# Attention and bilinear FFN on one core: Strassen for part of the first batch element, wider weight combinations, and probability sums made by accumulating transfers

## The chip, the cores and the metric

The kernel runs on one core of a Trainium2 chip. The metric is the time of one execution on the device, in microseconds, as the median of several runs. The profile is of one execution; its span is a little shorter than the time, since it begins with the first instruction that it shows.

In what follows PE is TensorE, DVE is VectorE, ACT is ScalarE, POOL is GpSimd and SP is the engine that issues most transfers. SBUF is the core's working memory, PSUM the memory into which PE writes.

## The reference

Four batch elements, eight heads, 768 positions, head size 64. Queries and keys are each put into one of 16 clusters by their largest cosine with the head's centroids, and a query attends only to keys of its own cluster. The result, 3072 rows of 512, goes through a bilinear feed-forward layer (FFN).

```python
q_assign = argmax(q_n @ c_n.T); k_assign = argmax(k_n @ c_n.T)
scores = where(q_assign == k_assign, q @ k.T / 8, -1e9)
x = softmax(scores) @ v              # (4, 8, 768, 64) -> (3072, 512)
out = (x @ w_a) * (x @ w_b) @ w_out  # 512 -> 1536 -> 512
```

The three FFN weights come as 64-bit floats and are turned into 32-bit ones on the core.

## The kernel before

**Attention.** Heads are worked on in pairs, 16 pairs in all, four per batch element (HP = 4). A pair has two halves of 384 queries (hf), and each half six units, one for each block of 128 keys (j = 0 to 5). A group, counted by g, is two units. For each group `score` makes both units' scores in PSUM (L554) and ACT takes the exponential into a tile pt (L563; four pt buffers, so a unit's exp overwrites the pt of four units earlier). In the next group `add_up` sums the probabilities of the half into a tile acc (L585), and `weigh` multiplies pt by v (L596). One or two groups after a half is complete, `denominators` sums acc over its partitions by a matmul with ones (L619), and `normalize` takes the reciprocal and multiplies it onto xT, the transposed attention output of the batch element (L653). In the first four pairs DVE makes all sums of `add_up` but the last block's, which PE takes in; in the other twelve POOL makes those of one head and the later ones of the other.

**FFN.** Once a batch element's xT is complete, `ffn_ready` puts its FFN, cut into pieces, into the queue `ffn`. The main loop over groups takes as many pieces per group as a credit of PE columns allows (PER_GROUP), and whatever is left runs after the last group. A piece's matmuls go through `in_halves` (L679), which makes two matmuls of 64 columns each. The up-projections of the last three batch elements use Strassen's scheme in Winograd's form (`ffn_ups`): seven products in place of eight for each pair of f-tiles (128 columns of w_a or w_b), from combinations of x (T1 to T4, `combine_x`) and of the weights (S1 to S4, L783, made by DVE one chunk of 128 at a time). ACT copies a product out of PSUM (L815), DVE adds further ones (L818), POOL multiplies the a and b sides (L824). The first batch element's up-projections are plain (`ffn_block`): each f-tile and half of the positions takes four chunks of 128 of the inner dimension. The down-projections use Strassen for all four.

**Weights.** 36 parts of 128x512 are loaded as 64-bit raw tiles (two buffers) and rounded by `round_w`: four DVE passes (L280 to L290) build a leading part and a rest, POOL adds them (L295), ACT takes the absolute value of the upper word (L294), and `flush_w` sets very small weights to zero on DVE (L302). `due` gives the group in which each part is rounded: eight in groups 1 to 22, the others from group 23.

**Order.** The order of instructions on each engine is the order in which the program is written; nothing is rescheduled. Small steps of `normalize` and of the next pair's preparation wait in the queue `todo` and are taken one after each FFN piece. A flag computed at the end decides whether a slow path (`long_path`) does everything again; with these inputs it doesn't run.

Of the kernel before, what the change touches and what calls it, by code (L numbers as in the profile page):

```python
# [28 lines left out]
SMALLEST = 1.125 * 2.0 ** -15  # L29

# [5 lines left out]
def kernel(  # L36
# [97 lines left out]
    with tc.If(redo > 0):  # L134
        with ExitStack() as slow:
            long_path(nc, tc, slow, c, q, k, v, out)


def short_path(nc, tc, ctx, c, cn, centroids_in, casts, n_far, q, k, v,
# [32 lines left out]
    sizep = pool("sizep", 2)  # L172
# [96 lines left out]
    flush = []  # L269

    def round_w(i):
        flush_w()
# [18 lines left out]
                                       in1=rest, op0=ALU.mult, op1=ALU.mult)  # L291

        size = sizep.tile([P, WN], FP32, name="size")
        nc.scalar.activation(out=size, in_=halves(FP32)[:, :, 1], func=AF.Abs)  # L294
        nc.gpsimd.tensor_tensor(out=w, in0=w, in1=rest, op=ALU.add)  # L295
        flush.append((w, size))

    def flush_w():

        while flush:  # L300
            w, size = flush.pop(0)
            nc.vector.scalar_tensor_tensor(out=w, in0=size, scalar=SMALLEST,  # L302
                                           in1=w, op0=ALU.is_ge, op1=ALU.mult)

    stat = zero.tile([P, 4 * NPAIR], FP32, name="stat")
# [151 lines left out]
    def prep_by_blocks(p):  # L457
# [47 lines left out]
        if p == HP:  # L505
            return [[lambda: across(0), lambda: across(1)], [sims_across],
                    assign[:2], assign[2:], [one_hot, one_hot_across], []]
# [3 lines left out]
    def prep_steps(p):  # L511
# [6 lines left out]
        if by_blocks(p):  # L518
            steps = prep_by_blocks(p)
            ready = [lambda s=s: todo.extend(s) for s in steps]  # L520
            ready[1] = both(lambda: prep_sim(p), lambda: load_v(p), steps[1][0],
                            lambda: todo.extend(steps[1][1:]))
            return ready
# [50 lines left out]
    def add_up(u):  # L574
        p, hf, j = where(u)
        if j == 0 or j == NJ - 1 and p < HP:
            return
        if j == 1:
            accs[p, hf] = accp.tile([P, 2, HB], FP32, name="acc")
        acc = accs[p, hf]  # L580
        for a in range(2):

            many = p >= HP and (a == 1 or j > 3)
            eng = nc.gpsimd if many else nc.vector
            eng.tensor_tensor(  # L585
                out=acc[:, a, :],
                in0=probs[u - 1][:, a, :] if j == 1 else acc[:, a, :],
                in1=probs[u][:, a, :], op=ALU.add)
# [39 lines left out]
    def normalize(p, hf):  # L628
# [21 lines left out]
        def apply():  # L650

            eng = nc.vector if (p, hf) == (HP - 1, 0) else nc.gpsimd
            eng.tensor_tensor(out=x, in0=x, in1=den, op=ALU.mult)  # L653
            unchecked.append((4 * p + 2 * hf + 1, inv))

        return [across, invert, back, apply]

    def check_inverses():
        while unchecked:
            n, inv = unchecked.pop()  # L660
            nc.scalar.activation(out=inv, in_=inv, func=AF.Copy,
                                 accum_out=stat[:, n:n + 1])

# [24 lines left out]
    def ffn_block(b, blk):  # L688

        box = {}  # L690
        t0 = blk * HB

        def up(w_sb, f):
            ps = in_turn()
            for ch in range(NCH):
                in_halves(ps[:, 0:HB], w_sb[:, ch, f * P:(f + 1) * P],
                          xTs[b][:, ch, t0:t0 + HB],
# [3 lines left out]
        def piece_a(f):  # L701
            if f == 0:
                box["h"] = hp_.tile([P, NF, HB], FP32, name="h")
            ps = up(wa_sb, f)
            box["a"] = hap.tile([P, HB], FP32, name="ha")
            nc.scalar.copy(out=box["a"], in_=ps[:, 0:HB])

        def piece_b(f):
            ps = up(wb_sb, f)
            nc.vector.tensor_tensor(out=box["h"][:, f, :], in0=box["a"],  # L710
                                    in1=ps[:, 0:HB], op=ALU.mult)

        ups = [(NCH * HB, lambda f=f, piece=piece: piece(f))
               for f in range(NF) for piece in (piece_a, piece_b)]
        return ups, box
# [11 lines left out]
    def room():  # L727
        if not W:
            W["raw"] = [rawp.tile([P, 2 * WN], FP32, name="raw") for _ in range(2)]
            W["size"] = [sizep.tile([P, WN], FP32, name="size") for _ in range(2)]  # L730
            W["comb"] = combp.tile([P, 2 * P], FP32, name="comb")
        return W["raw"], W["size"], W["comb"]
# [4 lines left out]
    def up_room():  # L737
        raw, size, comb = room()
        quarter = lambda t: t[:, 0:2 * HB].rearrange("p (c t) -> p c t", c=2)
        beside = lambda t: t[:, 2 * HB:].rearrange("p (c f) -> p c f", c=2)  # L740
        chunks = lambda t: [t[:, c, :] for c in range(2)]
        W["T3"], W["T2"] = chunks(quarter(raw[0])), chunks(quarter(raw[1]))
        W["T4"] = [t[:, 0:HB] for t in size]
        W["slots"] = [chunks(beside(raw[0])), chunks(beside(raw[1])),
                      chunks(comb.rearrange("p (c f) -> p c f", c=2)),
                      [t[:, HB:] for t in size]]

    def combine_x(b, c):
        if c == 0:
            up_room()  # L750
        x = xTs[b]
        x11, x12 = x[:, c, 0:HB], x[:, c, HB:S]
        x22 = x[:, c + 2, HB:S]
        t2, t3 = W["T2"][c], W["T3"][c]
        for out, l, r in ((t3, x22, x12), (x12, x12, x11), (t2, x22, x12)):
            nc.vector.tensor_tensor(out=out, in0=l, in1=r, op=ALU.subtract)

    def ffn_ups(b, h):

        x = xTs[b]  # L760
        X = {"11": [x[:, c, 0:HB] for c in (0, 1)],
             "T1": [x[:, c, HB:S] for c in (0, 1)],
             "21": [x[:, c, 0:HB] for c in (2, 3)],
             "22": [x[:, c, HB:S] for c in (2, 3)]}

        def combine_t4():
            for c in range(2):
                nc.vector.tensor_tensor(out=W["T4"][c], in0=X["21"][c],
                                        in1=W["T2"][c], op=ALU.subtract)

        def products(w_sb, i, is_a):
            N2 = NF // 2
            A = {m + n: [w_sb[:, c, f * P:(f + 1) * P] for c in cs]
                 for m, f in (("1", i), ("2", i + N2))
                 for n, cs in (("1", (0, 1)), ("2", (2, 3)))}
            box = {}

            def combine(name, l, r, op):
# [3 lines left out]
                for c in range(2):  # L782
                    nc.vector.tensor_tensor(out=dst[c], in0=l[c], in1=r[c], op=op)  # L783
# [16 lines left out]
            def product(name, l, r, start=True):  # L800
                ps = box[name]
                rhs = X[r] if r in X else W[r]
                for c in range(2):
                    in_halves(ps[:, 0:HB], A[l][c], rhs[c],
# [8 lines left out]
            def take(name, k, f):  # L813
                box[name] = place(k, f)
                nc.scalar.copy(out=box[name], in_=box["X"][:, 0:HB])  # L815

# [55 lines left out]
        parts = [products(w_sb, i, w_sb is wa_sb) for i in range(NF // 2)  # L872
                 for w_sb in (wa_sb, wb_sb)]
        pieces = []
        for n, (combinations, ps) in enumerate(parts):
            if n == 0:
                ps[0] = both(*combinations, ps[0])
                ps[2] = both(combine_t4, ps[2])
# [4 lines left out]
        return pieces  # L883
# [9 lines left out]
    def ffn_downs(b, h):  # L893
# [97 lines left out]
        def before():  # L991
            down_room()
# [19 lines left out]
    blocks = {}  # L1012

    def ffn_ready(p, hf):

        b, hp = divmod(p, HP)
        if hp < HP - 1:
            return
        if b > 0:
            if hf == 0:  # L1020
                return
            h = []
            for c in range(2):
                ffn.insert(len(ffn) - FREE_ROOM + c, (0, lambda c=c: combine_x(b, c)))
            ffn.extend(ffn_ups(b, h) + ffn_downs(b, lambda: h))
        elif hf == 0:
            blocks[0] = ffn_block(0, 0)
            ffn.extend(blocks[0][0][0:8])
        else:
            ups0, box0 = blocks[0]  # L1030
            ups, box = ffn_block(0, 1)
            for n in range(3):
# [370 lines left out]
```

## Time and profile before

| | |
|---|---|
| time, median of 3 | 1044.93 us (1044.05 to 1045.06) |
| span of the profile | 1042.1 us |
| PE busy | 1030.8 us |
| DVE busy | 658.7 us |
| ACT busy | 302.8 us |
| POOL busy | 334.1 us |
| transfers | 46.49 MB, 18.7% of the 16 DMA engines' span on the main queue |

Busy times of different engines overlap. A group row of the profile gives line, engine, operation, output and inputs, shapes and count, then the busy time of the whole group, the mean of one in ns, and the idle time of the engine just before these instructions with what ended most of it. An f32 matmul shows as two records.

### The profile page before, as it was taken

The page shows a single profiled execution, that of the slowest core. Times are in us where ns is not written, and L with a number is a line of the kernel's source. Part 1 is how long each engine was busy: PE and PEld are TensorE (multiplying, and loading weights), DVE is VectorE, ACT ScalarE, POOL GpSimd, SP SyncE. Part 2 cuts the span into 40 slices and gives each one's busy share as a digit, 9 for nine tenths or more (in the row PEclk, how much of TensorE's full clock was granted, in tenths as well). Part 3 has the DMA queues.
Part 4 walks back from the last instruction along what each step waited for, and adds up shares of the span by engine and source line. Part 5 has one row for each costly group of instructions (what it writes and reads, how often), then busy time and mean ns, then how long its engine had stood idle before and what let it go on. Part 6 is the DMA issues. An engine that isn't in the chain of part 4 may idle for free.

```text
span 1042.1 us, 17904 instructions
## 1 busy us (share of the span) xinstructions
PE 1030.8 (99%) x7158; PEld 500.5 (48%) x7158; DVE 658.7 (63%) x1314; ACT 302.8 (29%) x590; POOL 334.1 (32%) x310
## 2 busy tenths in 40 slices
PE   8999999999999999999999999999999999999997
PEld 5443444444445554444444555444444565444565
DVE  6777888889847447555546746755454835554652
ACT  5665333233322222332323122333232201111100
POOL 1111255555633332343443421444333310211100
PEclk9999999999999999999999999999999999999999
DMA  7334253525220121203020030300000000000001
GB/s 183 87 86 86 70 123 105 127 70 142 63 49 21 30 51 27 35 4 47 5 46 4 23 66 25 46 2 20 1 5 1 12 30 22 1 1 1 3 30 34
DMA packets 120523, 46.49 MB, mean 45 GB/s; under 512 B 106608, under 2 KB 115824, under 8 KB 120432
## 3 DMA queue, kind: packets, MB, share of 16 engines
q1 hardware_dynamic: 120016, 44.85, 18.7%
q8 instruction: 58, 0.95, 0.4%
q10 hardware_dynamic: 416, 0.43, 0.1%
q14 instruction: 33, 0.27, 0.1%
HBM read 37.78 MB, written 6.29 MB: 42 GB/s over the span
## 4 chain that ended last, share of the span: by engine, by line
PE 95%; DVE 2%; issue 1%; POOL 0%; DMA 0%; ACT 0%; DVEq 0%; POOLq 0%
PE m L679 63%; PE s L554 15%; PE O L596 13%; PE s L619 2%; PE m L619 1%; PE s L370 1%; PE m L370 0%; PE m L354 0%; DMA h<-in_q_dram 0%; DVE xT L910 0%; DVE raw L910 0%; PE m L430 0%; POOL xT L653 0%; PE m L384 0%; DVE h L919 0%
## 5 line engine op out<-in xcount | busy, mean ns | idle before, releaser
L563 ACT ACTIVATE pt<-s 128x768 f32<-128x768 f32 x192 | 145.3, 809 | 202.5 <-PE s L554 146.4
L585 POOL TENSOR_TENSOR acc<-acc,pt 128x384 f32<-128x384 f32 x144 | 155.6, 1100 | 60.0 <-ACT pt L563 45.9
L596 PE MATMUL O<-pt,v 128*64 128x384 f32 x768 | 145.1, 499 | 0.0
L554 PE MATMUL s<-qkT 64*128 64x384 f32 x768 | 139.7, 483 | 0.0
L824 POOL TENSOR_TENSOR h<-h,ha 128x384 f32<-128x384 f32 x54 | 56.1, 1041 | 255.6 <-DVE ha L818 255.1
L679 PE MATMUL m<-xT,wb_sb 128*64 128x384 f32 x672 | 116.4, 487 | 0.0
L679 PE MATMUL m<-xT,wa_sb 128*64 128x384 f32 x672 | 116.2, 487 | 0.2 <-DVE xT L653 0.2
L818 DVE TENSOR_TENSOR ha<-ha,m 128x384 f32<-128x384 f32 x72 | 39.6, 551 | 106.5 <-PE m L679 80.4
L815 ACT COPY h<-m 128x384 f32<-128x384 f32 x72 | 34.4, 478 | 184.9 <-PE m L679 184.9
L596 PEld LDWEIGHTS O<-pt,v 128*64 128x64 f32 x768 | 46.7, 136 | 85.7 <-issue 80.0
L679 PE MATMUL m<-wo_sb,h 128*64 128x256 f32 x768 | 86.7, 380 | 0.0
L554 PEld LDWEIGHTS s<-qkT 64*128 64x128 f32 x768 | 70.7, 187 | 31.2 <-issue 0.2
L818 DVE TENSOR_TENSOR h<-h,m 128x384 f32<-128x384 f32 x72 | 39.5, 549 | 72.3 <-PE m L679 46.9
L679 PE MATMUL m<-raw 128*64 128x384 f32 x432 | 78.9, 486 | 0.0
L653 POOL TENSOR_TENSOR xT<-xT,acc 128x384 f32<-128x384 f32 x31 | 32.5, 1048 | 143.2 <-DVE acc L646 143.0
L679 PEld LDWEIGHTS m<-xT,wb_sb 128*64 128x64 f32 x672 | 47.9, 137 | 61.2 <-issue 56.3
L679 PEld LDWEIGHTS m<-xT,wa_sb 128*64 128x64 f32 x672 | 48.0, 137 | 60.4 <-issue 55.6
L679 PEld LDWEIGHTS m<-wo_sb,h 128*64 128x64 f32 x768 | 55.0, 137 | 31.0 <-issue 5.0
L585 DVE TENSOR_TENSOR acc<-acc,pt 128x384 f32<-128x384 f32 x96 | 63.4, 687 | 2.3 <-ACT pt L563 1.0
L679 PE MATMUL m<-xT,h 128*64 128x256 f32 x576 | 64.5, 379 | 0.0
L679 PE MATMUL m<-xT,size 128*64 128x384 f32 x288 | 52.7, 487 | 0.0
L679 PEld LDWEIGHTS m<-xT,h 128*64 128x64 f32 x576 | 41.4, 137 | 22.3 <-issue 2.0
(168 smaller groups left out, 1312.3 us busy)
## 6 DMA issues: line engine op xcount, KB each, us to landing
raw<-in_moe_w_a_dram SPq DMA_DIRECT2D x12, 512.0 KB, 3.9
raw<-in_moe_w_b_dram SPq DMA_DIRECT2D x12, 512.0 KB, 3.6
raw<-in_moe_w_out_dram SPq DMA_DIRECT2D x12, 512.0 KB, 3.7
qk<-in_q_dram SPq DMA_DIRECT2D x48, 96.0 KB, 3.2
qk<-in_k_dram SPq DMA_DIRECT2D x48, 96.0 KB, 3.6
v<-in_v_dram SPq DMA_DIRECT2D x24, 192.0 KB, 3.8
out_dram<-rest SPq DMA_DIRECT2D x24, 128.0 KB, 1.7
v<-in_v_dram SPq DMA_DIRECT2D x4, 384.0 KB, 4.5
```

The lines of the kernel that those rows point to most:

```text
L370: nc.tensor.matmul(out=ps[32 * kq:32 * kq + 32, 0:HB], lhsT=cTb[:, hp, :], rhs=qkTs[p][:, kq * HB:(kq + 1) * HB], start=True, stop=True)
L554: nc.tensor.matmul(out=s[:, a, 0:HB], lhsT=Ts[p][r, S + j * P:S + (j + 1) * P], rhs=Ts[p][r, hf * HB:(hf + 1) * HB], start=start, stop=not ...
L563: nc.scalar.activation(out=pt, in_=s[:, :, 0:HB], func=AF.Exp, scale=SCALE)
L585: eng.tensor_tensor(out=acc[:, a, :], in0=probs[u - 1][:, a, :] if j == 1 else acc[:, a, :], in1=probs[u][:, a, :], op=ALU.add)
L596: nc.tensor.matmul(out=O_of[0][a * D:(a + 1) * D, 0:HB], lhsT=vs[p][:, a, j, :], rhs=probs[u][:, a, :], start=(j == 0), stop=(j == NJ - 1))
L619: nc.tensor.matmul(out=ps[a * D:(a + 1) * D, 0:HB], lhsT=ones, rhs=t[:, a, :], start=(n == 0), stop=(n == len(terms) - 1))
L653: eng.tensor_tensor(out=x, in0=x, in1=den, op=ALU.mult)
L679: nc.tensor.matmul(out=ps[half], lhsT=lhsT[:, half], rhs=rhs, **kw)
L815: nc.scalar.copy(out=box[name], in_=box["X"][:, 0:HB])
L818: nc.vector.tensor_tensor(out=box[name], in0=box[name], in1=box[bank][:, 0:HB], op=ALU.add)
L824: nc.gpsimd.tensor_tensor(out=to, in0=to, in1=box[name], op=ALU.mult)
```

## The change

Four things are changed together.

1. The up-projection of the first batch element: f-tiles 0 to 7, two thirds, now go through Strassen's scheme, as pairs (0,2), (1,3), (4,6) and (5,7); f-tiles 8 to 11 stay plain (`plain_ups`). T1 to T4 of this batch element lie in the part of the h tiles that the plain f-tiles fill later (`early_room`), and the first combinations are made in groups 16, 24 and 25 (`early_steps`). Its FFN is queued when the second half of the fourth pair is normalized, no longer in two steps from the first half on, and the columns per group are set for it.
2. Combinations of weights and of x are made in one DVE instruction for two chunks, 256 or 768 elements wide, in place of two.
3. In the last twelve pairs DVE makes the first sum of each half for both heads in one instruction, and the four further sums are transfers, issued from POOL, that add pt onto acc. In the first four pairs DVE sums both heads in one instruction.
4. Rounded weights are no longer flushed: ACT finds by a Relu with an accumulator, in `see_w`, whether a weight is that small; such a case would send the kernel to the slow path, which flushes. `see_w` also issues the next load. Parts from the ninth on are due from group 26.

```diff
+            size = spare()[0].bitcast(BF16)[:, 3 * WN:4 * WN]
+            nc.scalar.activation(out=size, in_=upper, func=AF.Abs)
+            n = 4 * NPAIR + i
+            nc.scalar.activation(out=size, in_=size, func=AF.Relu, scale=-STEEP,
+                                 bias=edge[:, 0:1], accum_out=stat[:, n:n + 1])
+            load_w(i + 2)
...
-            nc.vector.scalar_tensor_tensor(out=w, in0=size, scalar=SMALLEST,
-                                           in1=w, op0=ALU.is_ge, op1=ALU.mult)
...
-        for a in range(2):
-            many = p >= HP and (a == 1 or j > 3)
-            eng = nc.gpsimd if many else nc.vector
-            eng.tensor_tensor(
-                out=acc[:, a, :],
-                in0=probs[u - 1][:, a, :] if j == 1 else acc[:, a, :],
-                in1=probs[u][:, a, :], op=ALU.add)
+        if p < HP:
+            nc.vector.tensor_tensor(out=acc, in0=probs[u - 1] if j == 1 else acc,
+                                    in1=probs[u], op=ALU.add)
+            return
+        if j == 1:
+            nc.vector.tensor_tensor(out=acc, in0=probs[u - 1], in1=probs[u],
+                                    op=ALU.add)
+        else:
+            nc.gpsimd.dma_start(out=acc, in_=probs[u], accum_op=ALU.add)
...
+        N2, firsts = (NF // 2, range(NF // 2)) if b else (2, (0, 1, 4, 5))
...
-                for c in range(2):
-                    nc.vector.tensor_tensor(out=dst[c], in0=l[c], in1=r[c], op=op)
+                nc.vector.tensor_tensor(out=dst, in0=l, in1=r, op=op)
...
+            h = h_first
+            combine_x(0, "T2")
+            ffn.extend(ups_first + plain_ups(0, h, range(NF - 4, NF)))
+        ffn.extend(ffn_downs(b, lambda: h))
...
-        (UP + DOWN * 7 / 8, BG + 5.8), ((UP + DOWN) * 7 / 8, BG + 0.8),
+        (UP * 11 / 12 + DOWN * 7 / 8, BG + 2.8), ((UP + DOWN) * 7 / 8, BG + 0.8),
...
-        due.setdefault(23 + int((i - 8) / 1.5), []).append(i)
+        due.setdefault(26 + int((i - 8) / 1.5), []).append(i)
```

## The prediction

> **What bounds the kernel now.** I read four views, in this order: the page's busy shares and its chain; the windows (busy time of each engine by stage); the waits of TensorE alone; and single rows for prices.
>
> The page first. TensorE (PE) is busy for nearly the whole span, and the chain that ended last is PE for 95% of it, most of it on L679, the FFN's matmuls.
>
> ```profile
> span 1042.1 us, 17904 instructions
> ...
> PE 1030.8 (99%) x7158; PEld 500.5 (48%) x7158; DVE 658.7 (63%) x1314; ACT 302.8 (29%) x590; POOL 334.1 (32%) x310
> ...
> PE 95%; DVE 2%; issue 1%; POOL 0%; DMA 0%; ACT 0%; DVEq 0%; POOLq 0%
> ```
>
> The windows (columns: stretch, its length, PE, PEld, DVE, ACT, POOL busy, clock, DMA share, GB/s) show where PE is not full.
>
> ```profile
> 101.00:115.00 14.00, 11.74 (x70) 4.70 (x68) 11.65 (x24) 7.04 (x13) 2.39 (x3) 1.00 0.17 52
> 200.00:300.00 100.00, 100.00 (x630) 43.46 (x626) 83.65 (x123) 33.69 (x64) 59.27 (x49) 1.00 0.31 82
> 400.00:500.00 100.00, 100.00 (x632) 43.11 (x630) 55.45 (x122) 30.49 (x60) 38.67 (x38) 1.00 0.17 26
> 960.00:1042.10 82.10, 76.08 (x640) 45.54 (x636) 39.68 (x89) 5.76 (x14) 4.95 (x5) 0.98 0.07 21
> ```
>
> Of 1042.1 - 1030.8 = 11.3 us without PE, 6.0 lie at the end (last sums and stores), about 2.7 in the first 18 us, 2.3 between 101 and 115, 0.3 elsewhere. So shorter PE work counts in full, and all that a better DVE or POOL can give is the 2.3. The waits of PE name its cause: DVE late with a probability sum.
>
> ```profile
> PE m L619 <- DVE acc L585: 2.1, 1, 2.1
> ```
>
> The prices, from the chain in order of time (start, us, what) and the groups:
>
> ```profile
> 153.29 5.16 PE m L679 x32
> ```
>
> ```profile
> L585 POOL TENSOR_TENSOR acc<-acc,pt 128x384 f32<-128x384 f32 x144 | 155.6, 1100 | 60.0 <-ACT pt L563 45.9
> ...
> L585 DVE TENSOR_TENSOR acc<-acc,pt 128x384 f32<-128x384 f32 x96 | 63.4, 687 | 2.3 <-ACT pt L563 1.0
> ```
>
> 32 records in 5.16 us is 0.161 us each. An f32 matmul leaves two records: the program holds 336 matmuls of wa_sb on xT, the trace 672. So one f32 matmul of 64x384 costs 0.3225 us of PE.
>
> **What the skill says.** The Trainium skill, SBUF — State Buffer, Who interferes with whom: a DVE instruction with two SBUF inputs contends with GpSimd instructions that read SBUF. The trace agrees: a DVE sum of 384 takes 0.687 us beside POOL's sums, while an add of 384 with one input in PSUM takes 0.55. Moving POOL's sums away should help DVE. VectorE: DVE Perf Modes, The TRN2 errata — SBUF-src ops pay a fixed extra latency per instruction: wider is cheaper; each instruction pays a fixed cost. The trace agrees: 128 wide from SBUF 0.328 us, 384 wide 0.552. DMA: Bandwidth & Descriptors, Anatomy of one DMA — SWDGE (gpsimd) path: a GpSimd transfer takes some 2.0 us plus bytes over 436e3 per us, and its waits are held by the issuing sequencer. No transfer of this kind is in the trace of before. Collectives: The Full Stack, The bandwidth ceiling: the fold count and why AG ≠ RS ≠ AR: an adding transfer is slower because it reads two sources; no row shows that either.
>
> **The change, part by part.**
>
> 1. Strassen for f-tiles 0 to 7 of the first batch element. Plain, two f-tiles by two token halves take 2 x 2 x 4 chunks x 2 column halves = 32 matmuls for each of wa and wb; Strassen has 7 products x 2 chunks x 2 halves = 28. Four pairs of tiles times two weights save 8 x 4 = 32 matmuls. The instruction order of the two programs confirms it: the differences over all PE rows sum to -32 of 64x384. 32 x 0.3225 = 10.3 us off PE, and PE is the path. All else on PE has equal counts.
>
> 2. DVE. Removed: 136 sums of 384 (63.4 + 24.9 = 88 us) and the 36 flush passes of L302 (34.8 us). Added: 56 sums of 768 at about 0.9 to 1.1 us (0.552 plus 384 more at (0.552 - 0.328) / 256 per element gives 0.89; contended more), 56 us. Weight combinations: 288 of 128 wide (106 us by the L783 rows) become 176 of 256 wide at 0.44 to 0.6, some 90 us. Strassen adds for batch 0: 20 more DVE adds of 0.55, 11 us, and 4 combinations of x, 4 us. Sum: about 658.7 - 88 - 35 - 106 + 56 + 90 + 15 = 591 us. This is beside PE and gives only what PE now waits for: I credit the 2.1 us wait at 102 us, because it is a wait for a sum in the stage where the flush and the narrow sums crowd DVE (11.65 of 14 us).
>
> 3. ACT gets 36 Relu passes with an accumulator: 36 x (0.686 by the L294 row + 0.194 by the accumulator-read rows) = 32 us, and 16 - 4 = 12 more copies of 0.478. ACT goes from 303 to about 340 of 1042 us; hidden.
>
> 4. The FFN of batch 0 starts at group 26 instead of 23 and runs more columns per group (3726 for 3557). The three groups before have only attention, as the 20 before them, in which PE was full. No cost, if DVE keeps up.
>
> 5. Sums of the other twelve pairs by transfer: 168 POOL sums (155.6 + 29.6 us) go, 96 accumulating transfers of 384 KB come. Four per half-pair (j = 2 to 5) form a chain: each waits on POOL's own sequencer for the one before. Behind a waiting issue stand the h products (L824), weight adds (L295) and normalizations (L653); waiting for the transfers are exp (ACT: the pt buffer of four units earlier), the denominator matmul (PE itself) and the transposes of the sums (DVE).
>
> Length L of one transfer, bounded from both sides: the page's price gives 2.0 + 393216 / 436e3 = 2.9 us for a plain one (estimate). For two reads I take trace durations: 12 KB from SBUF to SBUF land in 1.8 us, 512 KB in 3.7; so 384 KB need about 1.4 us of data time beyond 1.8, twice that for two reads, plus issue: 1.8 + 2.9 + 0.4 = 5.1. I take 4.4, between them.
>
> Room: a group takes about 9.8 us in these stages (9.5 between 200 and 244 us, plus 169 columns at 2.58 us per 1536). With the first issue 1 us into a group, transfers 2 and 3 must be done before exp of the next group holds up ACT's copies for the FFN: PE does 1.72 + 1.44 of scores and weighing and two products of 1.29 before it needs such a copy, at 5.8 us; ACT needs 2.1 for two exps and a copy. So 1 + 2L <= 9.8 + 3.7, L <= 6.2. Transfers 4 and 5 begin at 9.8 + 1 and must end before the denominators, at 19.6 + 3.2: L <= 6.0. With 4.4 there is a margin of 3 us a group. A POOL that comes 3 us late at the group's start, behind weight adds that wait for DVE (groups 26 to 44), eats it. I charge 3 us in all for such waits, and for Strassen's batch 0 needing its combinations in time while DVE still rounds weights, which the plain form did not.
>
> Sum: -10.3 - 2.1 + 3.0 = -9.4; 1044.9 - 9.4 = 1035.5 us.
>
> **The rivals.**
>
> A. The forecast: PE loses 10.3 us and waits stay small; 1031.5 to 1040 us. For it: PE is 99% busy, the saving is a count. Against: the unseen transfer.
>
> B. The gain is largely eaten. Transfers of 5 to 6 us, or DVE's bursts in groups 26 to 44 (it was busy 84 to 91% there), stop PE for 0.5 to 0.8 us at half of the 24 half-pairs: with 0.65 us that is 8 us, 1040.5, and up to about 1045. For it: each transfer of qk also runs in the group in which transfer 5 ends, and DMA share was 0.85 for 8 us at such a load. Against: that load can only start when the transposes have freed qk, late in the group.
>
> C. The chain becomes the bound and the kernel is slower. With L = 6.5, transfers 4 and 5 end 2 x 0.5 = 1 us too late at each of 24 half-pairs: 24 us of new waits, so 1044.9 - 12.4 + 24 = 1056.5; with L = 7, 1080. For it: nothing in the trace has measured such a transfer, and two sources, generated descriptors and a semaphore in a row add up. Against: even the upper bound of L, 5.1, is under 6.0.
>
> D. Hidden anyway: the PE time comes back as waits for Strassen's combinations in batch 0 alone; 1042 to 1047 us. For it: batch 0 now depends on DVE while it rounds weights. Against: combinations are issued four to five products ahead, some 6 us.
>
> **How the numbers follow.** A 0.64, B 0.17, C 0.14, D 0.05. Faster by over 0.2% (below 1042.8): A and most of B, 0.78. Within 0.2%: the rest of B and part of D, 0.05. Slower: C and the rest, 0.17. The low end is PE's whole saving, the whole 2.1 us and 1 us more: 1031.5. The high end takes in B: 1045, which leaves about 0.17 above and 0.02 below.
>
> **What would show it right or wrong.** PE busy near 1020.5 us; no L619 wait of PE on DVE at about 100 us; the denominators' wait for the transfers near zero, accumulating transfers landing in 3 to 5.1 us; DVE near 590 us. Wrong if the waits of PE show L629 (the denominators' new line) stopped by transfers at most half-pairs, or exp waiting for transfers with PE empty behind it, or matmuls of batch 0 stopped by DVE combinations for more than a few us.

## The result, and the profile after

The change made the kernel slower: 1054.73 us median (1052.60 to 1054.98, 4 runs) against 1044.99 (1044.05 to 1045.67) for the kernel before, a ratio of 1.0089, 95% interval 1.0072 to 1.0107. The forecast was 1035.5 us with a range of 1031.5 to 1045.

The page of the changed kernel, the lines that answer to those of before:

```profile
span 1052.8 us, 17688 instructions
...
PE 1023.8 (97%) x7094; PEld 499.5 (47%) x7094; DVE 579.2 (55%) x1098; ACT 336.5 (32%) x674; POOL 254.1 (24%) x251
...
PE 80%; DMA 6%; DVE 6%; issue 4%; POOL 2%; ACT 2%; DVEq 0%; POOLq 0%; SPq 0%; ACTq 0%
```

The sums of busy time went where they were meant to go: DVE 579 us (forecast 591), ACT 337 (340), PE 64 records fewer, which is 32 f32 matmuls. But the chain is PE for 80% now and no longer 95%: PE stands idle for 1052.8 - 1023.8 = 29.0 us where it was 11.3.

The windows (stretch, length, PE, PEld, DVE, ACT, POOL, clock, DMA share, GB/s) show where:

```profile
101.00:115.00 14.00, 12.70 (x82) 5.32 (x80) 12.71 (x19) 7.59 (x15) 6.39 (x4) 1.00 0.13 30
115.00:135.00 20.00, 15.17 (x98) 6.18 (x96) 13.67 (x24) 9.14 (x19) 5.35 (x5) 0.97 0.77 146
135.00:200.00 65.00, 62.67 (x374) 26.14 (x376) 48.83 (x84) 29.71 (x62) 23.88 (x23) 0.96 0.59 129
200.00:300.00 100.00, 94.31 (x590) 41.17 (x588) 71.34 (x121) 47.61 (x97) 43.84 (x41) 1.00 0.64 143
400.00:500.00 100.00, 100.00 (x639) 43.62 (x636) 44.05 (x88) 30.68 (x61) 24.66 (x26) 1.00 0.48 83
```

Between 115 and 300 us, where the first batch element's up-projections run and DVE rounds the second part of the weights, PE loses 4.8 + 2.3 + 5.7 = 12.8 us; before, it was full from 115 to 200 and from 200 to 330. Between 400 and 500 it is full in both. The rest of the 17.7 us: 2.4 between 18 and 101 us, 0.4 before 18 and 0.4 between 300 and 400, 1.5 near 854, 1.4 behind the last store's issue, less 1.0 between 101 and 115 and 0.3 elsewhere (rounded, so the sum is not exact). PE busy itself is 3.3 us above the 1020.5 foreseen. The balance: -10.3 + 3.3 + 17.7 = +10.7 us of span.

What PE waited for (engine, mark, line, releaser: us in total, times, longest us):

```profile
PE m L692 <- DVE h L779: 5.6, 1, 5.6
PE s L629 <- DMA acc<-pt: 4.9, 4, 1.8
PE m L692 <- DVE ha L834: 2.5, 2, 2.3
PE s L563 <- ACT pt L572: 2.0, 6, 0.4
PE m L629 <- DVE acc L591: 1.3, 1, 1.3
```

Four kinds, then: a combination of x (L779, `combine_x`) and a sum of Strassen products (L834) late on DVE; the denominators waiting for an accumulating transfer; exps (L572) behind the new passes of `see_w` on ACT. The last row is the sum that I had seen late by 2.1 us; it is still late, by 1.3.

The longest wait, in the timeline of the changed kernel (start, us, engine, line, operation, output and inputs; in brackets the idle time before it and its releaser):

```profile
128.71 1.46 PE L692 MATMUL m<-h,comb 128*64 128x384 f32 x8
...
130.15 0.86 POOL L598 DMA_DIRECT2D acc<-pt  x1 [3.57 <-ACT pair L304]
...
130.72 1.58 POOL L292 TENSOR_TENSOR wa_sb<-wa_sb,rest 128x512 f32<-128x512 f32 x1
132.34 0.43 DVE L287 TENSOR_SCALAR rest<-wb_sb 128x512 int32<-128x512 int32 x1 [1.93 <-POOL wa_sb L292]
132.80 0.69 DVE L290 SCALAR_TENSOR_TENSOR rest<-raw,rest 128x512 f32<-128x512 uint32 x1
133.41 0.55 DVE L834 TENSOR_TENSOR h<-h,m 128x384 f32<-128x384 f32 x1
...
133.87 1.77 DVE L779 TENSOR_TENSOR h<-xT 128x768 f32<-128x768 f32 x1
```

Read it from below. PE wants T3, which is the row at 133.87. It stands on DVE behind the rounding of a weight part, which stood still for 1.93 us because the one `rest` buffer was free only after POOL's add of the part before, at 130.72; and that add stood on POOL behind a transfer issued at 130.15, 4.6 us after the one ahead of it (125.58). Releasers are inferred: the ACT instruction named there started at 129.30 and took 0.69 us, so it ended at 129.99, but the transfer has no use for what it writes. The transfer ahead, on whose sum this one adds, took 4.0 us and so landed near 129.6; what held POOL for the last half microsecond is not shown. T3 then took 1.77 us, and PE started again 5.62 us late.

The five microseconds after it show a second price:

```profile
135.00:140.00 5.00, 4.21 (x16) 1.84 (x18) 4.30 (x9) 0.48 (x1) 1.07 (x2) 0.50 0.67 171
```

The granted clock is 0.50. The Trainium skill, TensorE: Matmul & The Clock Gate, Part 1: The HAM clock gate, says that the clock falls to half after an idle window of some 3.4 us. This wait agrees: PE stopped at 130.17 us, and in short windows the clock is 0.50 from about 133.6 to 140.4 (waits shorter than 3.4 us, further below, were followed by the half clock too). PE worked for 4.6 us of that at half speed, which is 2.3 of the 3.3 us of extra PE busy time; the remaining 1.0 is not explained here, and t3_back_light below, whose matmuls are the same and whose clock stays at 1.00, has 1.2 of such an excess too.

The transfers themselves were about as forecast. The group of their issues (96 issues, total and mean ns, idle time before and its releaser) and the issue row (KB each, us to landing):

```profile
L598 POOL DMA_DIRECT2D acc<-pt x96 | 82.8, 862 | 261.1 <-DMA acc<-pt 161.5
...
acc<-pt POOLq DMA_DIRECT2D x96, 384.0 KB, 4.0
```

The median is 4.0 us (forecast 4.4); between 115 and 330 us it is 4.7, and the longest took 8.3. Seven of the 96 took more than the 6.0 us for which the prediction had room.

### The profile page after: what moved, and what is told of

It is laid out like the page before. It is cut to its first block, busy times and chain, and to the rows that moved or that the text cites. A ratio compares the mean times of both kernels' runs of the same rounds, so it can differ in the third digit from the quotient of the medians.

```text
span 1052.8 us, 17688 instructions
## 1 busy us (share of the span) xinstructions
PE 1023.8 (97%) x7094; PEld 499.5 (47%) x7094; DVE 579.2 (55%) x1098; ACT 336.5 (32%) x674; POOL 254.1 (24%) x251
## 4 chain that ended last, share of the span: by engine, by line
PE 80%; DMA 6%; DVE 6%; issue 4%; POOL 2%; ACT 2%; DVEq 0%; POOLq 0%; SPq 0%; ACTq 0%
PE m L692 54%; PE s L563 12%; PE O L606 10%; DMA acc<-pt 5%; PE s L629 1%; PE m L629 1%; PE s L378 1%; DVE acc L591 1%; ACT pt L572 1%; PE m L378 1%; POOL xT L661 0%; DVE acc L595 0%; POOL acc L598 0%; POOL h L840 0%; PE m L362 0%
## 5 line engine op out<-in xcount | busy, mean ns | idle before, releaser
L572 ACT ACTIVATE pt<-s 128x768 f32<-128x768 f32 x192 | 146.2, 808 | 191.1 <-PE s L563 142.6
L598 POOL DMA_DIRECT2D acc<-pt x96 | 82.8, 862 | 261.1 <-DMA acc<-pt 161.5
L840 POOL TENSOR_TENSOR h<-h,ha 128x384 f32<-128x384 f32 x66 | 72.8, 1110 | 214.6 <-DVE ha L834 213.7
L834 DVE TENSOR_TENSOR ha<-ha,m 128x384 f32<-128x384 f32 x88 | 48.1, 549 | 126.7 <-PE m L692 100.9
L834 DVE TENSOR_TENSOR h<-h,m 128x384 f32<-128x384 f32 x88 | 48.2, 547 | 100.9 <-PE m L692 73.5
L692 PE MATMUL m<-xT,wa_sb 128*64 128x384 f32 x480 | 83.7, 487 | 2.7 <-DVE ha L834 2.5
L692 PE MATMUL m<-xT,wb_sb 128*64 128x384 f32 x480 | 83.1, 486 | 0.4 <-DVE h L834 0.4
L661 POOL TENSOR_TENSOR xT<-xT,acc 128x384 f32<-128x384 f32 x32 | 35.2, 1099 | 133.4 <-DVE acc L656 84.1
L692 PE MATMUL m<-xT,pair 128*64 128x384 f32 x352 | 64.5, 487 | 0.0
L830 ACT COPY ha<-m 128x384 f32<-128x384 f32 x66 | 31.6, 478 | 98.8 <-PE m L692 93.2
L692 PEld LDWEIGHTS m<-xT,wa_sb 128*64 128x64 f32 x480 | 34.9, 137 | 46.1 <-issue 33.2
L692 PEld LDWEIGHTS m<-xT,wb_sb 128*64 128x64 f32 x480 | 34.6, 137 | 43.5 <-issue 37.0
```

What stands on the lines that cost most here:

```text
L572: nc.scalar.activation(out=pt, in_=s[:, :, 0:HB], func=AF.Exp, scale=SCALE)
L598: nc.gpsimd.dma_start(out=acc, in_=probs[u], accum_op=ALU.add)
L661: nc.gpsimd.tensor_tensor(out=x, in0=x, in1=den, op=ALU.mult)
L692: nc.tensor.matmul(out=ps[half], lhsT=lhsT[:, half], rhs=rhs, **kw)
L834: nc.vector.tensor_tensor(out=box[name], in0=box[name], in1=box[bank][:, 0:HB], op=ALU.add)
L840: nc.gpsimd.tensor_tensor(out=to, in0=to, in1=box[name], op=ALU.mult)
```

## The experiments

Two theories stood first. X: the transfers do it, because POOL holds the weight adds behind them and so holds DVE's rounding (the row at 130.72 above). Y: Strassen does it, because it makes PE depend on DVE while DVE rounds. All kernels are edits of the changed one unless said otherwise; T3 and T4 are made early in all whose names begin with t3, and in split_issue, adds_dve and half_steps_spread. The table has every result; the ratio is to the kernel before, with its 95% interval.

| run | Strassen in batch 0 | transfers | else | us | ratio |
|---|---|---|---|---|---|
| t3_early | yes | yes | T3, T4 early | 1050.53 | 1.0049 (1.0032 to 1.0066) |
| sums_late | yes | pairs 8 to 15 | | 1057.59 | 1.0118 (1.0100 to 1.0135) |
| sums_back | yes | no | | 1055.36 | 1.0103 (1.0085 to 1.0120) |
| plain_first | no | yes | | 1053.19 | 1.0082 (1.0065 to 1.0098) |
| plain_back | no | no | | 1045.55 | 1.0009 (1.0000 to 1.0018) |
| before_transfers | no | yes | on the kernel before | 1053.06 | 1.0077 (1.0060 to 1.0094) |
| split_issue | yes | yes | second transfer later | 1075.51 | 1.0289 (1.0268 to 1.0310) |
| adds_dve | yes | yes | weight adds on DVE | 1052.80 | 1.0072 (1.0056 to 1.0089) |
| t3_back | yes | no | T3, T4 early | 1054.02 | 1.0096 (1.0079 to 1.0113) |
| t3_back_light | yes | no | less rounding | 1037.62 | 0.9934 (0.9917 to 0.9950) |
| plain_back_light | no | no | less rounding | 1044.78 | 1.0002 (0.9993 to 1.0011) |
| t3_early_light | yes | yes | less rounding | 1041.57 | 0.9972 (0.9965 to 0.9979) |
| t3_back_spread | yes | no | earlier rounding | 1049.72 | 1.0050 (1.0033 to 1.0067) |
| t3_back_pool | yes | no | sums of pairs 4 to 7 on POOL | 1056.44 | 1.0112 (1.0085 to 1.0138) |
| t3_back_steps | yes | no | rounding in single steps | 1047.65 | 1.0033 (1.0023 to 1.0042) |
| t3_early_steps | yes | yes | rounding in single steps | 1068.48 | 1.0236 (1.0215 to 1.0257) |
| t3_back_steps_spread | yes | no | earlier rounding, in single steps | 1044.98 | 1.0006 (0.9997 to 1.0015) |
| half_steps_spread | f-tiles 0 to 3 | no | earlier rounding, in single steps | 1048.20 | 1.0037 (1.0023 to 1.0051) |

**The one long wait.** t3_early makes T3 and T4 of the first batch element right after T2:

```diff
-            combine_x(0, "T2")
+            for name in ("T2", "T3", "T4"):
+                combine_x(0, name)
...
-            elif n == 0:
-                ps[1] = both(ps[1], lambda: combine_x(b, "T3"))
-                ps[3] = both(lambda: combine_x(b, "T4"), ps[3])
```

> T3 and T4 of the first batch element are made right behind T2, before the weight rounding of group 26, so DVE no longer waits for POOL with T3 behind it. Both theories: PE's single wait of 5.6 us at 130 us goes, and with it the stretch of granted clock 0.5 to 0.96 behind it (about 3 us): 1054.7 - 8.6 = 1046, between 1044 and 1049. If the lost PE time is spread and only moves, it stays above 1051.

1050.53 us, between the two expectations (its eight executions ran from 1046.21 to 1052.35): the 5.6 us wait is gone, but only 4.2 us of time with it, and PE's waits for Strassen's sums (L834) grow from 2.9 to 5.5 us in all. It is one symptom, not the whole cause.

**Which part of the change.** Three runs put back the sums by instructions, in part or wholly (sums_late, sums_back), or the plain first batch element (plain_first); plain_back does both of the latter, and before_transfers adds all of part 3 of the change, the transfers and DVE's sums of both heads in one instruction, to the kernel before. In the plain versions the combinations of groups 16, 24 and 25 go too, and the columns per group are set for the plain form.

```diff
-        if j == 1:
-            nc.vector.tensor_tensor(out=acc, in0=probs[u - 1], in1=probs[u],
-                                    op=ALU.add)
-        else:
-            nc.gpsimd.dma_start(out=acc, in_=probs[u], accum_op=ALU.add)
+        for a in range(2):
+            many = a == 1 or j > 3
+            eng = nc.gpsimd if many else nc.vector
+            eng.tensor_tensor(
...
-            combine_x(0, "T2")
-            ffn.extend(ups_first + plain_ups(0, h, range(NF - 4, NF)))
+            ffn.extend(plain_ups(0, h, range(NF)))
```

> Transfers only in the last eight pairs; the four pairs of groups 24 to 47, in which weights are rounded, sum on DVE and POOL as before. Theory X (transfers stop POOL's queue, POOL's weight adds come late, the one buffer of the rest stops DVE, DVE stops PE): new waits between 115 and 330 us fall from some 13 us to under 4 and the clock stays at 1.00, 1036 to 1041. Theory Y (Strassen in the first batch element needs DVE while it rounds, whatever POOL does): 1048 or more, with PE waiting for DVE in groups 26 to 44.

> No transfers at all: sums of the last twelve pairs on DVE and POOL as before, all else as in the changed kernel. Theory X: within 2 us of the kernel with late transfers, 1036 to 1041, since after 330 us the transfers cost PE almost nothing. Theory Y: 1048 or more. If late transfers do cost, this is the faster of the two by over 2 us.

> First batch element's up-projection wholly plain, transfers and all else as in the changed kernel: PE has 10.3 us more to do. Theory X: POOL's queue is still stopped, but PE needs no combinations, so what stays is the waits for the sums themselves (some 5 us): 1047 to 1051. Theory Y: all new waits but these few go as well, so the two differ only by DVE waiting for POOL, which X sees stay (DVE's waits for L292 over 8 us in total) and Y sees gone.

> The kernel before with one part of the change, the transfers (and first sums of both heads in one instruction). Both theories: plain up-projections in the first batch element leave PE room, so only the waits of the denominators for transfers (about 5 us in all), 1.3 us more at the end behind the last store, less the 2.1 us at 102 us: 1047 to 1050. If the transfers in themselves slow PE, it is above 1052; if they are free, 1043 to 1045.

> Neither Strassen in the first batch element nor transfers: of the change there stay the wider combinations, the weights' check on ACT in place of the flush on DVE, the later start of the FFN and of the rounding. PE has the work of before. Both theories: no new waits after 115 us; 2.4 us of PE waiting for exps between 18 and 101 us (ACT's two passes per weight part stand ahead of them) against 1 us less at 105 us: 1045 to 1047. Above 1049, a part that neither theory names costs time.

X fell with sums_late and sums_back: without any transfer beside the first batch element the kernel is no faster. The waits of PE in sums_back:

```profile
PE m L694 <- DVE h L781: 7.2, 1, 7.2
PE m L694 <- DVE ha L836: 5.0, 2, 2.9
PE m L694 <- DVE xT L931: 2.4, 2, 2.0
```

All three are Strassen's combinations or sums, the first two of the first batch element, the third (L931) of its down-projection, which used Strassen before as well. The first wait is the one for T3, longer here without transfers (7.2 us) than with them (5.6), so it does not need the transfer that stood in front in the timeline above. PE is also busy for 1026.8 us, where the same matmuls take 1021.7 in t3_back_light below, so some 5 us are matmuls at a lower clock behind these waits.

But Y alone does not hold either: plain_first, with transfers and no Strassen, is nearly as slow, and so is before_transfers; both came out above the ranges that the two theories gave them (1047 to 1051 and 1047 to 1050), before_transfers in the one named for transfers that slow PE by themselves. In plain_first DVE still waits 9.3 us for POOL's weight adds, the sign that X named, but PE no longer waits for DVE after 115 us. It waits for transfers:

```profile
PE s L629 <- DMA acc<-pt: 5.3, 2, 4.1
```

The 4.1 us lie near 849 us, at the last denominators, long after the rounding. The trace shows one transfer issued there at 841.14, 12.2 us after the one ahead of it, behind a normalization (L661) for which POOL had stood idle for 10.4 us. PE then ran at a clock of 0.50 for some 5 us.

From plain_back's 1045.55, transfers alone cost 7.6 us, Strassen alone 9.8, both 9.2. The effects don't add. A likely reason is that transfers also take work from DVE (48.8 us busy between 135 and 200 us in the changed kernel, 60.2 in sums_back), which Strassen needs there: with T3 and T4 early, the version with transfers (t3_early, 1050.53) is even 3.5 us faster than the one without (t3_back, 1054.02). In before_transfers PE's main new row is

```profile
PE s L620 <- DMA acc<-pt: 6.9, 5, 2.7
```

so the transfers' cost is seen at the denominators (some 1.7 us of this run are not theirs: matmuls at half clock from 104 to 108 us, behind a wait for a sum made by DVE), with 0.5 to 1.5 us more at the end of the program in the kernels that have them. And plain_back settles the rest of the change: wider combinations, `see_w`, the later start and small moves that the list of four leaves out, such as the fourth pair's first normalization on POOL in place of DVE, are together worth nothing, within 0.2%.

**The chain through POOL.** Two runs loosen the hold of transfers on weight adds, both with T3 and T4 early. split_issue puts off each group's second transfer until three FFN pieces are issued; adds_dve moves the weight adds to DVE.

```diff
-            for u in before:
-                add_up(u)
+            add_up(before[0])
+            if before[1] < HP * UPP or before[1] % NJ == 1:
+                add_up(before[1])
+            else:
+                second_sum.append(before[1])
...
+                if done_here == 3:
+                    sum_second()
```

> As t3_early, and of a group's two transfers the second is issued after the group's third FFN piece and no longer right behind the first, so POOL does not stand in front of the weight adds and h products waiting for the first. Theory X: POOL's idle time before L598 that ends with a transfer falls from 161 us to under 40, DVE's waits for POOL's weight adds (12 us in the changed kernel) to under 3, PE's waits for DVE between 135 and 330 us (5.5 us in t3_early) to under 2: 1044 to 1047. Theory Y (the DVE's own load and order while it rounds): PE's waits for DVE stay over 4 us, 1049 to 1052.

```diff
-        nc.gpsimd.tensor_tensor(out=w, in0=w, in1=rest, op=ALU.add)
+        nc.vector.tensor_tensor(out=w, in0=w, in1=rest, op=ALU.add)
```

> As t3_early, with the 36 weight adds on DVE (L292), some 20 us more on DVE, two thirds of it in groups 26 to 44; POOL still waits for transfers, but DVE no longer waits for POOL's adds. Theory X: PE's waits for DVE between 135 and 330 us go under 2 us, 1045 to 1048. Theory Y: more load makes them longer than in t3_early, over 6 us, 1051 to 1055.

split_issue is the slowest of all, 1075.51 us, outside both expectations. DVE no longer waits for POOL's weight adds, POOL's idle time behind transfers falls only from 161.5 to 103.8 us, and PE pays at the denominators:

```profile
PE s L629 <- DMA acc<-pt: 21.8, 10, 5.4
```

The chain of four transfers has no room to start later: rival C's mechanism, reached by delaying the issue and not by the length of a transfer. adds_dve frees DVE of POOL and loads it with the adds, and nothing is won (1052.80 against 1050.53; the intervals overlap). PE's waits for Strassen's sums stay at 5.8 us there, where X expected under 2 and Y over 6.

**DVE's load while it rounds.** t3_back has Strassen, T3 and T4 early, and no transfers. Three edits take work away from DVE in the stage: t3_back_light leaves out the low part of the weights (L287, L290 and POOL's add, so the output uses the leading part alone), t3_back_spread rounds 14 parts before group 24 in place of 8 and the others more slowly, t3_back_pool makes all sums of pairs 4 to 7 on POOL.

```diff
-        nc.vector.tensor_scalar(out=rest.bitcast(INT32), in0=wi,
...
-        nc.vector.scalar_tensor_tensor(out=rest, in0=lo, scalar=2.0 ** -52,
-                                       in1=rest, op0=ALU.mult, op1=ALU.mult)
-        nc.gpsimd.tensor_tensor(out=w, in0=w, in1=rest, op=ALU.add)
```

> As sums_back (no transfers, Strassen in the first batch element), with T3 and T4 made right behind T2. The single wait of 7.2 us goes, and with it the stretch of lower clock behind it: 1055.4 - 7.2 - 3 = 1045, between 1043 and 1048. What stays are PE's waits for DVE while it rounds (some 7 us) and 2.4 us before 101 us.

> As t3_back, but the low part of the weights is left out (L287, L290 and POOL's add, about 1.1 us of DVE and 1.3 of POOL for each of 36 parts), so that DVE has some 20 us less to do in groups 26 to 44. If DVE's load while it rounds is what eats Strassen's gain in the first batch element: PE's waits for DVE after 115 us fall under 2 us, clock 1.00, 1035 to 1038. If something else eats it, 1042 or more.

```diff
-    due = {3 * i + 1: [i] for i in range(8)}
-    for i in range(8, len(w_parts)):
-        due.setdefault(26 + int((i - 8) / 1.5), []).append(i)
+    due = {}
+    for i in range(14):
+        due.setdefault(1 + int(1.7 * i), []).append(i)
+    for i in range(14, len(w_parts)):
+        due.setdefault(26 + int((i - 14) / 1.25), []).append(i)
```

> As t3_back, with 14 weight parts rounded before group 24 in place of 8 and the others at 1.25 per group in place of 1.5. DVE's load: between 135 and 330 us from 85 to 80%, before 101 us from 70 to 85%. If the load while it rounds decides, PE's waits for DVE after 115 us halve, but ACT's passes before 101 us cost more: 1040 to 1045.

> As t3_back, with all sums of the four pairs of groups 24 to 47 on POOL: 2 us less for DVE in every third group's span of 30 us, 3.3 us more for POOL. If DVE's load decides: 1041 to 1045. If POOL (its weight adds and h products behind ten sums) takes over: over 1047.

t3_back missed its expectation by far: 1054.02 us. The single wait of 7.2 us is gone, but the time is not clearly better than that of sums_back (1055.36; the intervals overlap), for PE now waits for the sums of products instead (L836; L928 is a combination for the down-projection):

```profile
PE m L694 <- DVE ha L836: 5.3, 2, 3.2
PE m L694 <- DVE h L836: 5.1, 2, 2.7
PE m L694 <- DVE xT L928: 2.0, 1, 2.0
```

The window from 135 to 200 us, first of t3_back, then of t3_back_light:

```profile
135.00:200.00 65.00, 59.96 (x362) 24.93 (x364) 62.79 (x94) 29.33 (x60) 37.45 (x32) 0.97 0.38 99
```

```profile
135.00:200.00 65.00, 63.09 (x394) 26.65 (x392) 51.94 (x86) 33.16 (x67) 26.99 (x25) 1.00 0.43 109
```

DVE is busy 62.8 of 65 us in the first and 51.9 in the second; PE gains 3.1 us in this stage and keeps its clock. The whole is 16.4 us faster, 7 us below the kernel before. About 5 us of that is PE's busy time (1026.8 us in t3_back, 1021.7 here, for the same matmuls), the clock's part. The control, plain_back_light, has the same work left out and no Strassen:

> plain_back (no Strassen in batch 0, no transfers) with the low part of the weights left out, as in t3_back_light. If the light run gained because Strassen then works: nothing waits for DVE here anyway, so 1044.5 to 1046 us, as plain_back. If it gained for another reason (rounding itself held PE up): 1035 to 1040 us.

1044.78 us, as plain_back. So the missing work is worth nothing by itself: it is Strassen that gains by it, 1044.78 - 1037.62 = 7.2 us of its 10.3. The edit takes two DVE passes and POOL's add away and halves the block of passes, so by itself it doesn't tell DVE's load from POOL's add or from the order of work. t3_back_spread went in the right direction and less far than expected. t3_back_pool gained nothing (1056.44, in the range expected if POOL takes over; the interval overlaps with that of t3_back): DVE has 84 instructions in the stage and not 94, but they take 59.09 / 84 = 0.70 us each in place of 62.79 / 94 = 0.67, and POOL is fuller (43.4 us in place of 37.5).

And the transfers on top of the lighter rounding:

> t3_early (Strassen and transfers, T3 and T4 early) with the low part of the weights left out. If the transfers cost time by themselves (denominators wait, end of the program): 1041 to 1046 us, that is 4 to 8 above t3_back_light's 1037.6. If they cost only through POOL's and DVE's rounding: 1037 to 1039 us.

1041.57 us, 3.9 above t3_back_light, with

```profile
PE s L622 <- DMA acc<-pt: 3.1, 3, 1.6
```

So beside Strassen and the lighter rounding the transfers cost some 4 us, at the denominators and at the end. This and the 7.6 us from plain_back to plain_first differ in two things, the rounding and Strassen, so where the other 3.6 come from is not shown; the one long wait of plain_first, at 849 us, is outside the rounding.

**Load or order.** A full DVE need not stop PE: before the change it was busy 59.1 of 65 us in the same stage, and PE was full:

```profile
135.00:200.00 65.00, 65.00 (x412) 28.10 (x409) 59.14 (x84) 22.31 (x41) 35.44 (x29) 1.00 0.46 114
```

What differs is who waits for what DVE does next. The timeline of DVE in t3_back ahead of one wait of PE:

```profile
219.14 0.72 DVE L280 TENSOR_SCALAR wb_sb<-raw 128x512 int32<-128x512 int32 x1
219.89 0.69 DVE L283 SCALAR_TENSOR_TENSOR wb_sb<-raw,wb_sb 128x512 int32<-128x512 int32 x1
220.69 0.43 DVE L287 TENSOR_SCALAR rest<-wb_sb 128x512 int32<-128x512 int32 x1
221.15 0.69 DVE L290 SCALAR_TENSOR_TENSOR rest<-raw,rest 128x512 f32<-128x512 uint32 x1
221.76 0.55 DVE L836 TENSOR_TENSOR ha<-ha,m 128x384 f32<-128x384 f32 x1
```

The last row adds a product out of PSUM and frees the bank that PE needs (PE waited 3.24 us for it). It stands behind the four passes of one part, 2.6 us in a block. t3_back_steps issues these passes singly, one after each FFN piece, with the same work (its parts from the ninth on are due a group earlier):

```diff
-                round_w(i)
+                rounding.append(round_w(parts.pop(0)))
+            if rounding:
+                for _ in rounding[0]:
+                    if ffn:
+                        break
...
-        due.setdefault(26 + int((i - 8) / 1.5), []).append(i)
+        due.setdefault(25 + int((i - 8) / 1.5), []).append(i)
```

> t3_back with a weight part rounded in single DVE operations, one after each FFN product, in place of four in a block (and the parts from the ninth on due one group earlier); the work is the same. Order theory (Strassen's adds stand behind blocks of 3 us): waits of PE for DVE in 130 to 330 us fall from 15 to under 5 us; 1037 to 1044 us. Throughput theory (DVE is full, 63 of 65 us): the waits stay, 1049 to 1056 us.

> t3_early with the rounding in single operations: the change as it was meant. Order theory: waits for DVE and POOL in the rounding stage mostly vanish, those for transfers stay: 1041 to 1047 us. Throughput theory: 1050 us, as t3_early.

The window of t3_back_steps from 135 to 200 us, its busy PE, and its waits:

```profile
135.00:200.00 65.00, 63.66 (x396) 26.91 (x394) 62.70 (x99) 33.71 (x69) 41.11 (x32) 1.00 0.37 94
...
PE 1021.9 (98%) x7094; PEld 494.7 (47%) x7094; DVE 642.7 (62%) x1146; ACT 335.8 (32%) x674; POOL 360.2 (34%) x323
...
PE m L699 <- DVE ha L845: 5.3, 3, 3.1
PE m L699 <- DVE h L787: 2.9, 1, 2.9
```

DVE is as full as in t3_back (62.7 us), but PE has 63.7 us and not 60.0; between 115 and 135 us, though, it has 17.1 and not 19.7, for a combination of x is late again (the row of L787). The time fell by 6.4 us to 1047.65, between the two expectations. How it fell was not what the order theory said: PE's waits for DVE between 115 and 330 us go only from 12.4 us in the profile of t3_back to 10.1, and not under 5. The larger part is the clock: PE is busy for 1021.9 us in place of 1026.8. This part varies from one execution to the next (14 ran from 1046.15 to 1050.98, with a mean clock from 1.000 to 0.992). The three slowest of them, with a clock of 0.992, still took about 3 us less than those of t3_back with 0.994, so a part of the gain is not clock. With transfers the same edit is much slower, 1068.48, far above both expectations: POOL's weight adds now wait for passes that come later, the next transfer stands behind them (one add waited 2.84 us for DVE with a transfer behind it, shortly before a denominator came 4.7 us late), and

```profile
PE s L634 <- DMA acc<-pt: 15.8, 6, 4.7
```

This is the coupling of X, running the other way.

The last two put both remedies together, without transfers, and halve Strassen's share:

> t3_back with both remedies: rounding in single operations and 14 parts rounded before group 24. If order and load are two causes whose parts add up: 1054.0 - 6.4 - 4.3 = 1043 us, 1041 to 1045. If they are one cause: no better than the better of the two, 1046 to 1049 us.

> the same with two of the four pairs' worth of Strassen in batch 0 (f-tiles 0 to 3; 4 to 11 plain), which has 5.2 us less to gain and half of DVE's combinations and adds. If waits grow faster than the gain: 1040 to 1043 us, below both kernels. If each pair of tiles loses alike: about halfway between the other run and 1045.5.

1044.98 us for t3_back_steps_spread: the parts add nearly (6.4 and 4.3 foresaw 1043.3), which speaks for order and load as two causes. But that only brings the time back to that of the kernel before; no version with the whole computation came out faster. half_steps_spread missed both expectations: with two of the four pairs of f-tiles plain, 5.2 us of saving are gone and the time rises by 3.2, so by this difference the other two pairs keep most of their gain in this arrangement. It keeps one 3.8 us wait near 134 us for `combine_x`, behind POOL's normalization of xT; the same wait in t3_back_steps_spread is 2.2 us. No run has the earlier rounding without Strassen, so what this rounding costs by itself is not shown.

## Why the prediction was wrong

1. Strassen's saving was right as a count: 32 matmuls went. With the rounding made lighter, 7.2 us of the 10.3 reach the time.
2. DVE's sum was right (579 us for 591), though two readings beside it were means over quick and slow instructions: the rows L783 have a median of 0.28 us where 0.328 was read, and the DVE sums of 384 one of 0.55 where 0.687 was read, so most of those did not run slower beside POOL. The credit of 2.1 us was mis-sized: that wait is now 1.3 us, and 0.8 us is what came of it.
3. ACT was not quite hidden: the new passes stand ahead of exps in the first 100 us, and PE waits 2.0 us for these, six times 0.3 to 0.4. This alone eats the 0.8 us of step 2; plain_back, which has both, shows no gain.
4. The later start cost nothing that the runs show.
5. The length of a transfer (4.0 us for 4.4) was right at the median, and in part by luck: it was a point between two estimates, and doubling the data time for two reads gave 5.1. That L stays under 6 held for 89 of 96. Rival C's time came, but not for its reason. Wrong was the small price put on what happens around a transfer: some take up to 8.3 us, and some are issued late because POOL holds other work ahead of them, as at 841 us in plain_first. The transfers alone cost 7.6 us without Strassen, and 4 with Strassen and the lighter rounding.

The step that failed is the last term of the sum: "I charge 3 us in all for such waits, and for Strassen's batch 0 needing its combinations in time while DVE still rounds weights". The runs put 7.6 us on the transfers alone, and 9.8 on Strassen alone, which means that its 10.3 us were given back and some 10 more taken. Rival D named this mechanism and gave it 1 chance in 20 with a limit of 1047 us, as though waits could eat no more than the saving. The limit had no ground. In the profile of sums_back the new waits for DVE come to 14.6 us (7.2, 5.0 and 2.4), and the lower clock behind them to some 5, against a saving of 10.3. The reason given against D, that combinations are issued four to five products ahead, looked at the wrong instruction. Besides combinations, the sums that empty PSUM banks (L834) hold PE up, and these can't be made ahead; each stands behind whatever block of rounding was issued before it.

The profile of before had what was needed. DVE was busy 59 of 65 us in the stage; I named this under rival B, and priced it at 0.5 to 0.8 us at half of the half-pairs. It was harmless because DVE owed PE little: between 115 and 330 us, 24 instructions (L710) that empty a bank for the plain up-projections, one for two products of 2.58 us (8 matmuls of 0.3225). In t3_back there are 44 in the same stretch and 32 combinations of weights, and a Strassen product takes half as long.

What stays open: why the transfers cost 7.6 us in plain_first and 4 in t3_early_light, and how this divides between POOL's order and slower transfers; how much of Strassen's loss is DVE's load, how much order, and how much POOL's adds, which were taken from POOL by themselves only beside transfers (adds_dve); and whether an order of POOL and DVE exists in which both parts of the change pay.

## What to carry to other kernels

When a change shortens the bounding engine's work by making it depend on another engine, price the other engine in that stage and not over the span, and list what stands in front of the new operation in its in-order queue: a block of 2.6 us of work that nobody waited for turned into waits of 2 to 3 us here. Test this by taking unrelated work from that engine, with a control that lacks the new dependence. A wait can cost more than the saving that brought it, so "the gain is eaten" is not a limit. Count PE's busy time as well as its waits: here some 5 us of the loss were matmuls at a lower clock, which a list of waits does not show.

## What the runs showed of the hardware

- Around one idle stretch of 5.6 us PE's granted clock was 0.50 for 6.8 us, 4.6 of them with PE at work, as said above. Waits shorter than the idle window cited there did this too, but not always: in t3_back waits of 2.7 us, of 2.1 and 3.2 close together, and of 2.0 us were each followed by about 3.4 us at 0.50; in the profiled execution of t3_back_steps single waits of 2.9 and 3.1 us, and in t3_back_light waits of 1.1, left it at 1.00.
- DVE's combinations of 128x256 with both inputs in SBUF took 0.41 to 0.42 us alone and often 1.2 to 1.25 beside POOL's adds (L800 in t3_back), in one case 2.6 (L804 in t3_early_steps). The Trainium skill, SBUF — State Buffer, Who interferes with whom, says that such instructions contend with GpSimd's reads; the trace agrees and shows a factor of three in most such cases.
- An accumulating transfer of 384 KB from SBUF to SBUF landed in 3.9 us at best, 4.0 at the median and 8.3 at worst; its issue took POOL 0.86 us. Kernels with such transfers ended 5.7 to 6.7 us after the last store had been issued, those without 5.1 to 5.3, though in the changed kernel the last such transfer was issued at 851.6 us.
